# One output tile per attention step: spreading filler matmuls anew in a fused attention and FFN kernel on one Trainium2 core

## The chip, the core and the metric

The kernel runs on one core of one Trainium2 chip. The core has five engines that work beside each other and meet through semaphores: TensorE (PE in the profile; PEld is its loading of weights), VectorE (DVE), ScalarE (ACT), GpSimd (POOL) and SyncE (SP), which here only issues DMAs. Matrix products go to PSUM banks, all other tiles lie in SBUF, and inputs, outputs and some intermediates in HBM. The metric is the device time of one execution in microseconds, the median over runs.

## The reference

```python
def _A_ref(x, wqkv, wo):            # H = 32 heads of Dh = 16, S = 2048, D = 512
    q, k, v = (x @ wqkv) split in heads
    p = softmax(q k^T * Dh**-0.5)
    return (p v, heads joined) @ wo

def _B_ref(x, w_gate, w_up, w_down):   # F = 1792
    return (silu(x @ w_gate) * (x @ w_up)) @ w_down

xn = _layernorm(x)
s = _A_ref(xn, A_wqkv, A_wo)
g = silu(_B_ref(xn, B_w_gate, B_w_up, B_w_down))
return x + s * g
```

All data are fp32. Where TensorE multiplies, the kernel splits most operands in a high and a low part and sums three products (high by high, high by low, low by high).

## The kernel before

**Stages.** A prologue (to about 162 us of the span) normalises x, projects queries, keys and values, and writes them to HBM. Then comes the attention, 256 steps, in which everything else is hidden: the FFN and the output projection. A short tail ends it.

**The attention.** A unit `u` is four heads (`g` = u // 4) by one block of 512 queries (`b` = u % 4): 32 units of 8 steps each. The number of a step is `now = u * 8 + kp`, 0 to 255. A step handles 256 keys. On PE it issues, in program order (L801 to L823):

1. for `i = 0`: two score products `j = 0, 1` (L810, two matmuls each, into `score[0]` and `score[1]`), each followed by an exponential on ACT (L812). A score tile can be written again only when its exponential has read it;
2. `catch_up()`: what the last filler tile left to do (`after`), and then the value products of the *previous* step (`values(prev)`, L367, 16 records);
3. for `i = 1`: two more score products and exponentials;
4. `share()`: filler matmuls for this step;
5. if the previous step ended a unit, `finish` of that unit on DVE: transpose, reciprocal, product (L374 to L381), for odd `g` one more transpose (L388) and, for the last `g` and b > 0, a split into two parts (`split_o`, L261 and L262).

Step 0 has no value products, since nothing precedes it.

**The filler.** `queue` holds generators whose every `next` issues a *pair*: two matmuls of 64 rows into the banks `bankx` and `banky` (`both`, L174). Per FFN block there are 14 gate/up tiles of 24 pairs, in two groups (8 and 6), and after each group four down tiles of 24 or 18 pairs. Then come four tiles of 9 pairs for output block 3 (without its last part), and twelve output tiles of 12 pairs for blocks 0 to 2, here called O0 to O11. When a tile's last pair is issued, its readers follow in program order: a tanh on ACT (L203) and products on DVE (L204, L205) for a gate/up tile, adds on DVE (L222 to L227) for a down tile, and for an output tile the bank reads L340 and L341 on DVE, two products on POOL (L317, L318) and a store. The next tile writes the same two banks, so it waits until DVE has read them.

**The plan.** `plan()` writes the list `shares`: how many pairs each step issues. `tile_of(n, parts)` gives a tile of n pairs to that many steps in equal parts. `FIRST` pairs of the first step go between the scores of `i = 0` and `i = 1` (L816). A gate/up tile has 3 steps of 8. A down tile of 24 pairs has 3 steps of 8, or 2 of 12: `HALVED` counts sixteenths, so 9 of the 16 such tiles have two steps. `OUT_PARTS` gives the output tiles O0 to O10 one step of 12 or two of 6; O11 follows after the last step. All 256 steps have an entry. The first entries belong to tile 1, since tile 0 runs in the prologue.

**Work bound to a step's number.** `finish(29)` comes in step 240 and `finish(30)` in step 248. `load_gate` (L348), in step 248, loads four gate tiles and four tiles of x; `gate_rest` (L355 to L358), in step 251 and behind `share()`, runs eight operations on DVE with them. `out_steps` (L293) loads the parts of blocks 0 to 2 for the output tiles and splits them on DVE, two per step, when the queue has come so far; `load_gates` in it loads gates and x (L286, L287). `store_gate` and `next_out` (L176, L245) run in `catch_up` of the step after a down tile of the last group: a tanh on ACT (L178), a product on DVE (L179), the split of a part of `wo` (L241, L242) and of a part of block 3 (L261, L262), which the four tiles of 9 pairs read.

Of the kernel before, what the change touches and what calls it, by code (L numbers as in the profile page):

```python
# [25 lines left out]
NB = 4  # L26
TB = S // NB
NT = TB // P
DT = D // P
# [9 lines left out]
RING = NB + 1  # L39
DC = D // HALF  # L40
LIMIT = 160.0
FIRST = 5
HALVED = 9
OUT_PARTS = (2, 2, 1, 1, 1, 1, 1, 2, 1, 2, 2)
EPS = 1e-5
QSLOT = (0, 1, 0)
KSLOT = (0, 0, 1)
# [3 lines left out]
def tile_block(ctx: ExitStack, tc: tile.TileContext, x, wqkv, wo, w_gate, w_up, w_down, out):  # L51
# [51 lines left out]
    def load_k(g, c, i=None):  # L103
        load_rows(kst[(g * NB + c) % RING if i is None else i],
                  k_d[:, g * 64:(g + 1) * 64, c * TB:(c + 1) * TB], KSLOT)

    def load_q(u, i=None):
        g, b = divmod(u, NB)
        load_rows(qst[u % 2 if i is None else i], q_d[:, g * 64:(g + 1) * 64, b * TB:(b + 1) * TB], QSLOT)

    def load_shift(u):
        for h in range(2):
            sp.dma_start(qst[u % 2][h * HALF:h * HALF + 2].bitcast(F32),
                         sh_d.rearrange("(s u) (j h t) -> u h s j t", s=2, j=2, h=2)[u, h])

    def load_v(g, c):
        sp.dma_start(vst[(g * NB + c) % RING], v_d[g][:, c * CT:(c + 1) * CT])
# [38 lines left out]
    def catch_up():  # L156
        while after:
            after.pop(0)()
# [134 lines left out]
    def out_steps():  # L293
        for _ in range(min(2, len(splits))):
            b, c = splits.pop(0)
            split_o(lhs[b, c], parts_o[b, c])
            ready[b] += 1
        for b in range(NB - 1):
            if b not in stage and len(queue) <= (NB, NB, 2)[b]:
                for c in range(DT - 1):  # L300
                    load_out(b, c)
                stage[b] = now
            if b in stage and not b and (b, 1) not in stage and now > (u0 + b) * steps:
                load_out(b, DT - 1)
                stage[b, 1] = now
            if b in stage and (b, 2) not in stage and now > stage[b]:
                splits.extend((b, c) for c in range(DT - 1))
                stage[b, 2] = now
            if (b, 1) in stage and (b, 5) not in stage and now > stage[b, 1]:
                splits.insert(0, (b, DT - 1))  # L310
                stage[b, 5] = now
            if len(queue) <= NB - 1 - b and (b, 4) not in stage:
                load_gates(b)
                stage[b, 4] = now
# [33 lines left out]
    def load_gate():  # L348
        last.extend(on[:3] + [one.tile([P, D], F32, tag="wdr", name="last")])
        for t in range(NT):  # L350
            r = rows[(NB - 1) * NT + t]
            sp.dma_start(gate[t], g_d[r])
            sp.dma_start(last[t], x[r])

    def gate_rest():  # L355
        for t in range(NT):
            dve.scalar_tensor_tensor(facc[:, t], facc[:, t], 0.5, gate[t], op0=ALU.mult, op1=ALU.mult)
            dve.tensor_add(facc[:, t], facc[:, t], last[t])  # L358


    def values(item):
        u, kp, probs = item
        v, a = vst[(u // NB * NB + kp * 2 // CT) % RING], acc[u % 2]
        for i in range(2):
            kt = 2 * kp + i
            for h in range(4):
                mm(a[h * 32:h * 32 + DH + 1], v[:, kt % CT, h * (DH + 1):(h + 1) * (DH + 1)],  # L367
                   probs[2 * i + h // 2][:, h % 2], start=kt == 0, stop=kt == KT - 1, skip_group_check=True)
# [14 lines left out]
    def finish(u):  # L383
        g, b = divmod(u, NB)
        normalise(u, 0, TB)
        if g % 2:
            o2 = late.tile([P, TB], F32, tag="o2", name="o2")
            dve.transpose(o2, on[b])  # L388
            if g < NG - 1 or not b:
                (pool if g < NG - 1 else sp).dma_start(o_d[g // 2, b], o2)  # L390
            else:
                whole = (wd, hh)[b - 1].rearrange("p f j t -> p (f j) t")
                lhs[b, DT - 1] = whole[:, 2 * (DT - 1)], whole[:, 2 * DT - 1]
                split_o(lhs[b, DT - 1], o2)
                ready[b] += 1
# [14 lines left out]
    now = -1  # L410

    def fill(n):
        nonlocal given
        while n > 0 and not blocked():
            next(queue[0][1])
            queue[0][2] -= 1
            if not queue[0][2]:
                queue.pop(0)
            n -= 1
            given += 1  # L420
# [3 lines left out]
    shares = []  # L424

    def plan():
        def tile_of(n, parts):
            shares.extend([n // parts] * parts)

        halved = 0  # L430
        for i in range(2 * NB):
            nf = GROUPS[i % 2].stop - GROUPS[i % 2].start
            for _ in range(nf - (i == 0)):
                tile_of(3 * DC, 3)
            for t in range(NT):
                if nf == FG:
                    halved += HALVED
                    tile_of(3 * nf, 3 - halved // (NB * NT))
                    halved %= NB * NT
                else:  # L440
                    tile_of(3 * nf, 2)
        for _ in range(NT):
            tile_of(3 * (DT - 1), 1)
        for parts in OUT_PARTS:
            tile_of(3 * DT, parts)
        shares[0] -= FIRST

    def blocked():
        return not queue or queue[0][0] is not None and ready[queue[0][0]] < DT

    def share():
        if not blocked() and shares:
            fill(shares.pop(0))
# [337 lines left out]
    now = 0  # L791
    split_hidden()
    plan()
    prev = None

    exps = []
    settled = mybir.DependencyInfo(mybir.DependencyClass.Sync, mybir.DependencyReason.DATA)
    for u in range(units):
        g, b = divmod(u, NB)
        q = qst[u % 2]  # L800
        for kp in range(steps):  # L801
            now = u * steps + kp
            probs = []
            for i in range(2):
                kt = 2 * kp + i
                k, kc = kst[(g * NB + kt // CT) % RING], kt % CT
                for j in range(2):
                    for h in range(2):
                        r = slice(h * HALF, h * HALF + NROW)
                        mm(score[j][:, h], k[r, j, kc * P:(kc + 1) * P], q[r, j], start=True, stop=True)  # L810
                    pr = ppool.tile([P, 2, TB], F32, tag="pr", name="pr")
                    exps.append(act(pr, score[j], AF.Exp, scale=0.25))  # L812
                    if i == 0 and j == 1 and now:
                        tc.add_manual_dep(exps[-1].ins, exps[-3].ins.name, settled, reason="order of the slots' writes")
                    probs.append(pr)
                if now == i == 0:  # L816
                    fill(FIRST)
                if i == 0:
                    catch_up()
                if i == 0 and prev:  # L820
                    values(prev)
            old, prev = prev, (u, kp, probs)
            share()  # L823
            if old and old[1] == steps - 1:
                finish(old[0])
            if kp == 0:
                if u + 1 < units:
                    load_q(u + 1)
                    load_shift(u + 1)
            if g + 1 < NG and (b == 0 and kp == 0 or b == NB - 1 and kp in (2, 4, 6)):  # L830
                load_k(g + 1, kp // 2)
                load_v(g + 1, kp // 2)
            out_steps()
            if now == (units - 1) * steps:
                load_gate()
            if now == (units - 1) * steps + 3:
                gate_rest()
# [66 lines left out]
```

## Time and profile before

| | |
|---|---|
| three runs | 1448.03, 1449.05, 1448.93 us; median 1448.93 |
| profiled execution | 1448.02 us, span in the trace 1446.2 us |
| granted TensorE clock | 0.998 of full speed |
| exponentials (L812), mean of one | 1023 ns, 1024 of them |
| value products (L367), records | 4096 |
| filler matmuls of the gate/up tiles, mean of one | 392 ns |

In the views of the profile a line begins with the start in us from the span's start and the duration in us, then the engine, the line of the program (L810), the operation, and the tiles as out<-in. In brackets stands how long the engine was idle before it and what ended the idle time. The chain of waits is followed back from the last instruction; a row of it is a stretch in which that instruction set the pace. "PE bankx L174 x2" would be two filler matmuls. An engine with a q behind its name (SPq) is its instruction queue.

### The profile page before, as it was taken

The numbers are of one execution on the slowest core, as the hardware profiler recorded it, in microseconds if no ns is written. First come the engines' busy times: TensorE is split into PE (matmuls) and PEld (weight loads), VectorE is DVE, ScalarE is ACT, GpSimd is POOL, SyncE is SP. The second block draws the span as 40 slices with busy tenths as digits, with TensorE's granted clock in tenths as the row PEclk, the third lists the DMA queues.
The fourth block names the chain that finished last, engine by engine and source line by source line (L and its number), as shares of the span: only waits on it lengthen the run. The fifth ranks groups of instructions, "written<-read, shape, count | busy, mean of one in ns | idle before, by whom it ended". The sixth has DMA issues, their size and how long they took to land.

```text
span 1446.2 us, 26820 instructions
## 1 busy us (share of the span) xinstructions
PE 1430.6 (99%) x11237; PEld 804.3 (56%) x11237; DVE 538.9 (37%) x905; ACT 1110.2 (77%) x1235; POOL 88.7 (6%) x103
## 2 busy tenths in 40 slices
PE   8999999999999999999999999999999999999997
PEld 7777655555555555555555555555555555555554
DVE  6543344223423433134323431333253412434445
ACT  5733588778888888788888877888888877887774
POOL 3200200000000000000000000000000000000153
PEclk9999999999999999999999999999999999999999
DMA  6778652032264330242624311245424212315262
GB/s 209 265 243 243 162 118 62 23 80 69 71 150 118 96 78 20 49 107 71 143 67 127 80 42 34 78 107 112 116 67 125 56 25 47 83 36 173 76 202 78
DMA packets 127093, 148.64 MB, mean 103 GB/s; under 512 B 12540, under 2 KB 79100, under 8 KB 126196
## 3 DMA queue, kind: packets, MB, share of 16 engines
q1 hardware_dynamic: 121764, 126.19, 33.8%
q0 software_dynamic: 4912, 20.12, 3.8%
q8 instruction: 91, 1.49, 0.4%
q10 hardware_dynamic: 288, 0.52, 0.1%
q14 instruction: 38, 0.31, 0.1%
HBM read 106.94 MB, written 39.85 MB: 101 GB/s over the span
## 4 chain that ended last, share of the span: by engine, by line
PE 96%; ACT 2%; DVE 1%; issue 0%; DMA 0%; DVEq 0%; ACTq 0%
PE acc L367 32%; PE bankx L174 30%; PE score L810 20%; PE ps L578 6%; PE banky L174 4%; PE ps L580 3%; ACT pr L812 2%; PE acc L555 0%; PE bankx L330 0%; DMA facc<-in_A_x_dram 0%; DVE y L861 0%; DVE xn L550 0%; ACT xt L558 0%; DVE y L864 0%; PE bankx L585 0%
## 5 line engine op out<-in xcount | busy, mean ns | idle before, releaser
L812 ACT ACTIVATE pr<-score 128x1024 f32<-128x1024 f32 x1024 | 992.3, 1023 | 233.6 <-PE score L810 232.9
L367 PE MATMUL acc<-pr,vst 128*17 128x512 f32 x4096 | 489.2, 595 | 0.0
L810 PE MATMUL score<-qst,kst 50*128 50x512 f32 x2048 | 355.1, 422 | 3.4 <-ACT pr L812 2.4
L810 PEld LDWEIGHTS score<-qst,kst 50*128 50x128 f32 x2048 | 177.5, 185 | 268.4 <-ACT pr L812 230.6
L174 PE MATMUL bankx<-fx,guh 64*128 64x512 f32 x896 | 288.6, 392 | 0.0
L174 PE MATMUL banky<-fx,guh 64*128 64x512 f32 x896 | 288.6, 392 | 0.0
L367 PEld LDWEIGHTS acc<-pr,vst 128*17 128x17 f32 x4096 | 94.0, 97 | 235.7 <-issue 234.8
L204 DVE SCALAR_TENSOR_TENSOR ga<-th,bankx 128x512 f32<-128x512 f32 x56 | 38.5, 687 | 460.2 <-ACT th L203 460.2
L174 PEld LDWEIGHTS bankx<-fx,guh 64*128 64x128 f32 x896 | 165.9, 185 | 33.5 <-issue 0.3
L174 PE MATMUL banky<-fx,gul 64*128 64x512 f32 x448 | 175.4, 392 | 0.0
L174 PE MATMUL bankx<-fx,gul 64*128 64x512 f32 x448 | 175.4, 392 | 0.0
L174 PEld LDWEIGHTS banky<-fx,guh 64*128 64x128 f32 x896 | 166.0, 185 | 3.5
L174 PE MATMUL bankx<-wd,hh 64*128 64x512 f32 x672 | 165.5, 389 | 0.0
L174 PE MATMUL banky<-wd,hh 64*128 64x512 f32 x672 | 165.4, 389 | 0.0
L174 PEld LDWEIGHTS bankx<-wd,hh 64*128 64x128 f32 x672 | 124.1, 185 | 25.0
L174 PEld LDWEIGHTS banky<-wd,hh 64*128 64x128 f32 x672 | 124.2, 185 | 2.1
L174 PEld LDWEIGHTS bankx<-fx,gul 64*128 64x128 f32 x448 | 82.9, 185 | 17.7
L174 PEld LDWEIGHTS banky<-fx,gul 64*128 64x128 f32 x448 | 82.9, 185 | 1.7
L578 PE MATMUL ps<-xt,wh 128*128 128x512 f32 x256 | 80.7, 396 | 0.0
L135 DVE TENSOR_TENSOR gul<-gur,guh 128x1024 fp32r<-128x1024 f32 x56 | 68.6, 1225 | 2.4 <-DVE guh L134 0.5
L222 DVE COPY facc<-bankx 128x512 f32<-128x512 f32 x16 | 11.1, 691 | 153.1 <-PE banky L174 130.0
L390 POOL DMA_DIRECT2D o_d<-o x12 | 7.5, 622 | 824.7 <-DVE o L388 632.2
(147 smaller groups left out, 1065.0 us busy)
## 6 DMA issues: line engine op xcount, KB each, us to landing
gur<-in_B_w_gate_dram SPq DMA_DIRECT2D x56, 256.0 KB
gur<-in_B_w_up_dram SPq DMA_DIRECT2D x56, 256.0 KB
wdr<-in_B_w_down_dram SPq DMA_DIRECT2D x56, 256.0 KB
kst<-k_d SPq DMA_DIRECT2D x192, 64.0 KB
qst<-q_d SPq DMA_DIRECT2D x192, 64.0 KB
fx<-xt_d SPq DMA_DIRECT2D x24, 512.0 KB
q_d<-parts SPq DMA_DIRECT2D x16, 512.0 KB
k_d<-parts SPq DMA_DIRECT2D x16, 512.0 KB
```

The lines of the kernel that those rows point to most:

```text
L135: dve.tensor_sub(lo, raw, hi.bitcast(F32))
L174: mm(bank, lhs[h], rhs[h], start=start, stop=stop)
L204: dve.scalar_tensor_tensor(ga, th, 1.0, bankx, op0=ALU.add, op1=ALU.mult)
L222: dve.tensor_copy(facc[:, t], bankx)
L367: mm(a[h * 32:h * 32 + DH + 1], v[:, kt % CT, h * (DH + 1):(h + 1) * (DH + 1)], probs[2 * i + h // 2][:, h % 2], start=kt == 0, stop=kt == ...
L390: (pool if g < NG - 1 else sp).dma_start(o_d[g // 2, b], o2)
L578: mm(ps, w, a[:, c], start=n == 0, stop=n == 3 * DT - 1)
L580: mm(ps, a[:, c, tokens], w, start=n == 0, stop=n == 3 * DT - 1)
L810: mm(score[j][:, h], k[r, j, kc * P:(kc + 1) * P], q[r, j], start=True, stop=True)
L812: exps.append(act(pr, score[j], AF.Exp, scale=0.25))
```

## The change

Four places change, all in what is issued when; no instruction is added or removed.

```diff
-FIRST = 5
-HALVED = 9
-OUT_PARTS = (2, 2, 1, 1, 1, 1, 1, 2, 1, 2, 2)
+FIRST = (5, 2, 2)
+HALVED = 3
...
-            for _ in range(nf - (i == 0)):
-                tile_of(3 * DC, 3)
+            for f in range(nf - (i == 0)):
+                tile_of(3 * DC, 3 if i or f else 2)
...
-        for parts in OUT_PARTS:
-            tile_of(3 * DT, parts)
-        shares[0] -= FIRST
+        for _ in range(NB * NT - NT - 1):
+            tile_of(3 * DT, 1)
+        shares[0] -= sum(FIRST[:2])
+        shares[1] -= FIRST[2]
...
-                if now == i == 0:
-                    fill(FIRST)
+                    if now == i == 0 and j:
+                        fill(FIRST[0])
+                    elif (now, i, j) in ((0, 1, 0), (1, 0, 0)):
+                        fill(FIRST[1 + now])
```

The pairs per step, as the two plans give them (the entries of step 0 and 1 include those placed between scores):

| | before | after |
|---|---|---|
| tile 1 | steps 0 to 2: 8, 8, 8 | steps 0 and 1: 12, 12 |
| down tiles of 24 pairs in two steps | 9 of 16 | 3 of 16 |
| the last FFN tile ends in | step 235 | step 240 |
| block 3, four tiles of 9 | steps 236 to 239 | steps 241 to 244 |
| O0, O1 | 240, 241 and 242, 243 (6 each) | 245, 246 |
| O2 to O6 | 244 to 248 | 247 to 251 |
| O7 | 249, 250 (6 each) | 252 |
| O8 | 251 | 253 |
| O9, O10 | 252, 253 and 254, 255 (6 each) | 254, 255 |

In the opening, step 0 issues two scores, 5 pairs, a score, 2 pairs, a score, 5 pairs; step 1 a score, 2 pairs, a score, the value products of step 0, two scores, 10 pairs. Before, these were two scores, 5 pairs, two scores, 3 pairs; and two scores, the value products, two scores, 8 pairs.

Since the list of the steps' own work stays where it is, the filler tiles move past it: `finish(29)` now stands behind the last pair of the last FFN tile in DVE's program, and `gate_rest` behind O6 and one split, ahead of O7. In SP's program the load of the queries of unit 31 moves ahead of the loads for blocks 0 and 1, and the loads of the x rows for block 1 come to stand just before those of `load_gate`.

## The prediction

> **What bounds the kernel now.** I read the page first: busy times, then the chain that ended last.
>
> ```profile
> span 1446.2 us, 26820 instructions
> ...
> PE 1430.6 (99%) x11237; PEld 804.3 (56%) x11237; DVE 538.9 (37%) x905; ACT 1110.2 (77%) x1235; POOL 88.7 (6%) x103
> ...
> PE 96%; ACT 2%; DVE 1%; issue 0%; DMA 0%; DVEq 0%; ACTq 0%
> ```
>
> PE is the bound and the change removes none of its matmuls, so only stretches where PE waits can be won or lost. The chain in order of time, over the last hundred microseconds, shows what a step costs (a stretch that starts with "acc L367" is the value product of one step; from one to the next is one step).
>
> ```profile
> 1351.65 1.95 ACT pr L812 x2
> ...
> 1356.45 1.95 ACT pr L812 x2
> ...
> 1358.45 0.50 PE score L810 x2
> 1358.95 1.84 PE acc L367 x16
> 1360.79 0.45 PE score L810 x2
> ...
> 1361.26 1.95 ACT pr L812 x2
> ...
> 1374.31 1.84 PE acc L367 x16
> 1376.15 0.66 PE score L810 x4
> ...
> 1380.07 1.84 PE acc L367 x16
> ...
> 1412.30 0.46 PE score L810 x4
> ...
> 1424.69 1.95 ACT pr L812 x2
> ```
>
> A step with 12 pairs (1374.31 to 1380.07) takes 5.76 us and consists of PE alone: 1.84 for the values, 0.66 and 0.46 for the two groups of scores, 2.80 for the pairs. A step with 6 pairs (1356.45 to 1361.26) takes 4.81, and there the chain passes through two exponentials: the second score tile is not free until they end, and six pairs don't fill that time.
>
> The same view at the opening:
>
> ```profile
> 163.30 3.78 ACT pr L812 x4
> ...
> 167.63 1.84 PE acc L367 x16
> ...
> 172.47 1.84 PE acc L367 x16
> ...
> 177.31 1.84 PE acc L367 x16
> ```
>
> A step with 8 pairs takes 177.31 - 172.47 = 4.84. So a pair costs (5.76 - 4.84) / 4 = 0.23, a step without pairs 4.84 - 8 x 0.23 = 3.00, and six pairs would take 4.38 if PE set the pace. Since the steps (256) and the pairs stay the same in number, everything linear cancels: what counts is where a step is longer than 3.00 + 0.23 n.
>
> **1. The halved output tiles: a gain.** Nine steps of 6 pairs end in such a wait (first 1351.65, last 1424.69; the tenth, step 255, has no scores behind it). Each loses 4.81 - 4.38 = 0.43, together 3.9 us. Afterwards every step has at least 8 pairs. Those put into FFN down tiles make steps of 8, which run at PE's pace already. Bounds: 0 if another wait takes the same place, 3.9 if none does. I take 3.9, since the 12-pair and 8-pair rows show no exponential in the chain.
>
> **2. The pairs between scores at the opening: a gain.** No value product exists in step 0, and PE waits for exponentials:
>
> ```profile
> 165.29 0.18 PEld L810 LDWEIGHTS score<-qst,kst 50*128 50x128 f32 x2 [0.73 <-ACT pr L812]
> ...
> 167.12 0.19 PEld L810 LDWEIGHTS score<-qst,kst 50*128 50x128 f32 x2 [0.73 <-ACT pr L812]
> ...
> 173.05 1.23 DVE L135 TENSOR_TENSOR gul<-gur,guh 128x1024 fp32r<-128x1024 f32 x1
> 177.51 0.69 DVE L204 SCALAR_TENSOR_TENSOR ga<-th,bankx 128x512 f32<-128x512 f32 x1 [3.23 <-ACT th L203]
> 178.30 0.69 DVE L205 SCALAR_TENSOR_TENSOR ga<-ga,banky 128x512 f32<-128x512 f32 x1
> ```
>
> Ahead of the first value product stand 8 pairs now and 5 + 2 + 5 + 2 = 14 afterwards; six pairs are 1.39 us of work put into idle time. Going through the new order with these rows: the second score of step 0 still starts at 165.29 and streams for half of 0.46, five pairs run to about 166.8, a score and two pairs to 167.5, and the last score (free since the four exponentials ended at 167.08) to 167.7. The value product thus starts some 0.1 us later than 167.63: a gain of 1.3. Bounds: 0 if the delayed score holds the exponentials up by as much as is won, 1.39 at best.
>
> A cost comes with it. The first tile's 24 pairs now end in step 1 (10 pairs), and the next tile starts one step earlier: its first pair is due at 167.73 + 3.00 + 2.31 (next values, 173.04) + 1.84 + 0.66 = 175.54. The banks must have been read by L204 and L205 by then, and VectorE has L135 until 174.28; L204 and L205 after it take 178.99 - 177.51 = 1.48, so to about 175.7. With the restart I put 0.3 (0 if VectorE's order gives way, 0.8 if the weight load of the new tile is late too).
>
> **3. The end of the FFN meets the end of a unit: a loss.** Steps 240, 248 and 251 do fixed work by their number: `finish(29)`, `finish(30)`, `gate_rest`. The tiles move past them. The last down tile ended in step 235 and now ends in step 240, where `finish(29)` follows on VectorE, ahead of the next step's `store_gate` and `next_out`. Where VectorE stands, and PE's wait for it in the first output step of block 3:
>
> ```profile
> 1328.36 0.69 DVE L227 TENSOR_TENSOR y<-banky,y 128x512 f32<-128x512 f32 x1
> 1330.30 0.69 DVE L179 SCALAR_TENSOR_TENSOR y<-th,y 128x512 f32<-128x512 f32 x1 [1.25 <-ACT th L178]
> ...
> 1332.43 0.69 DVE L262 TENSOR_TENSOR part<-pair,part 128x512 fp32r<-128x512 f32 x1
> 1333.71 0.69 DVE L344 COPY facc<-bankx 128x512 f32<-128x512 f32 x1 [0.59 <-PE banky L174]
> ...
> 1340.18 0.42 DVE L261 CAST hh<-hh 128x512 fp32r<-128x512 f32 x1
> ...
> 1341.25 0.42 DVE L261 CAST hh<-hh 128x512 fp32r<-128x512 f32 x1
> ...
> 1352.44 0.71 DVE L374 STREAM_TRANSPOSE o<-acc 128x512 f32<-128x512 f32 x1
> ...
> 1355.75 0.42 DVE L261 CAST wd<-wd 128x512 fp32r<-128x512 f32 x1
> ...
> 1413.81 0.68 DVE L357 SCALAR_TENSOR_TENSOR facc<-facc,hh 128x512 f32<-128x512 f32 x1
> 1414.52 1.65 DVE L358 TENSOR_TENSOR facc<-facc,on 128x512 f32<-128x512 f32 x1
> 1416.10 1.76 DVE L357 SCALAR_TENSOR_TENSOR facc<-facc,hh 128x512 f32<-128x512 f32 x1
> ...
> 1421.58 0.69 DVE L340 TENSOR_SCALAR y<-bankx 128x512 f32<-128x512 f32 x1 [0.33 <-PE banky L174]
> 1422.38 0.69 DVE L341 SCALAR_TENSOR_TENSOR y<-banky,y 128x512 f32<-128x512 f32 x1
> ```
>
> ```profile
> PEld bankx L174 <- DVE part L261: 1.0, 1, 1.0
> ```
>
> PE waited 1.0 us there already, for the split of L261/L262 whose end (1333.12) releases the last pair. `finish` with its split takes 1355.75 - 1352.44 = 3.31. VectorE was free at about 1328.97 (0.61 after L227's start, as its operations follow each other) and idle until the tanh came; with `finish` in that place L179 starts at 1332.28 instead of 1330.30. All behind it, and PE's wait, move by 1.98: a loss of 2.0. Bounds: 1.3 (part of it beside PE's own work) to 3.3 (all of `finish`).
>
> **4. `gate_rest` stands before a bank release that has no second step left: a loss.** In step 251 it runs behind tile O8 and takes 1421.58 - 0.33 - 1413.81 = 7.44 until VectorE asks for O9, which takes two steps: nobody waited. Afterwards it runs behind O6, with one more split (1341.25 - 1340.18 = 1.07) ahead of it, and O7 ends one step of 5.76 later. With step 251's pairs ending at 1412.30: O7 ends at 1418.06, its release L340 could start at 1418.17, but VectorE comes to it at 1413.81 + 1.07 + 7.44 = 1422.3 and has read the second bank 0.80 + 0.69 later, at 1423.8. PE wants the banks for O8 at 1418.06 + 0.46 + 1.84 + 0.66 = 1421.0. From the end of such a split to the end of the pair behind it row 1333.71 shows about 0.48, so O8's first pair ends near 1424.3 instead of 1421.25: a loss of 2.9 (with the unrounded rows). What is late next is only O8's own release, with a full step for 1.5 us of work.
>
> Lower bound 0.9: two of the eight operations took 1.65 and 1.76 instead of 0.69, beside these on POOL.
>
> ```profile
> 1413.98 1.65 POOL L317 TENSOR_TENSOR y<-y,gates 128x512 f32<-128x512 f32 x1 [2.69 <-DVE y L341]
> 1415.71 1.61 POOL L318 TENSOR_TENSOR pair<-y,pair 128x512 f32<-128x512 f32 x1
> ```
>
> Without those 2.0 us the loss is 0.9. The upper bound, 4, has the loads of rival B a microsecond late. I take 2.9, as POOL does the same two products for O6 at the same place. [...]
>
> POOL's own work, 1.65 + 1.61 at most for a tile, fits a 5.76 step, so one tile a step doesn't make POOL the bound.
>
> **Sum.** -3.9 - 1.3 + 0.3 + 2.0 + 2.9 = 0.0. The profiled execution took 1448.02 (span 1446.2 and 1.8 around it), the median of the runs is 0.9 above it: I predict 1448.9. Each wait removed comes back as a wait on VectorE.
>
> **The rivals.**
>
> A, the VectorE waits don't appear: only 1 and 2 count, 1448.9 - 5.2 = 1443.7. For it: VectorE is busy only 37%. Against it: the order of its instructions puts `finish(29)` and `gate_rest` ahead of the operations PE waits for, and in the rows above its operations follow their program order. Chance 0.15.
>
> B, slower: `gate_rest` waits for its loads. The gate and x rows are queued on SP behind the load of x for the next block, which waits for an output store:
>
> ```profile
> 1386.62 0.33 SPq L287 DMA_DIRECT2D pair<-in_A_x_dram  x1
> ```
>
> That came 7.0 after O3 ended (0.46 before 1380.07). O3 now ends in step 248, where `load_gate` is issued, so the eight loads leave behind it; `gate_rest` starts 3 x 5.76 + 2.6 = 19.9 after O3. This leaves 12.9 us for eleven loads. From the point where they need more, every microsecond is one of PE: 4 us late gives 1452.9. Chance 0.12.
>
> C, the opening gives nothing because the exponentials of step 1 are pushed back by what PE wins: 1448.9 + 1.3 = 1450.2, still no change. Chance 0.10.
>
> [...] Chance 0.08.
>
> **How the numbers follow.** The forecast keeps 0.55, with a range of its own of 1447 to 1450.5 from the bounds of 2, 3 and 4. I give 1445.0 to 1451.5, which takes in C and D and leaves out A and B but for their mild ends. What this measurement can tell from no change is about 0.2%, 2.9 us: below 1446.0 is faster, A and a tail of the forecast, 0.17; above 1451.8 is slower, B, 0.12; no change is 0.71.
>
> **What would show it.** Right: no step with an exponential in the chain among the output steps; the first value product near 167.7 with 14 pairs ahead; PE waiting about 3 us for L262's counterpart in step 241, and about 3 us for VectorE's bank reads in step 253, behind a run of eight `gate_rest` operations. Wrong: step 241 or 253 at its plain length (A), `gate_rest` waiting on a DMA (B), the first value product after 168.5 (C), or output steps above 5.8 us throughout, which would mean that POOL or the loads can't follow one tile a step.

## The result and the profile after

| | before | after |
|---|---|---|
| median, 16 runs each | 1448.2 us (1447.68 to 1449.05) | 1451.95 us (1447.5 to 1453.15) |
| span of the profiled execution | 1446.2 us | 1450.8 us |
| granted TensorE clock in it | 0.998 | 0.995 |

The ratio after to before is 1.002, with a 95% interval of 1.0014 to 1.0027: slower by 3.75 us, 0.26%, and 0.45 us above the stated range. The 16 runs after fall into three groups: two took 1447.5 and 1447.65 us, with a granted clock of 0.999, two about 1449.4 with 0.998, and twelve 1450.9 to 1453.15 with 0.995 or 0.996.

The page of the changed kernel, the same rows as before:

```profile
span 1450.8 us, 26829 instructions
...
PE 1434.1 (99%) x11237; PEld 807.6 (56%) x11237; DVE 540.2 (37%) x905; ACT 1111.1 (77%) x1235; POOL 88.0 (6%) x103
...
PE 97%; DVE 2%; ACT 0%; issue 0%; DMA 0%; DVEq 0%
```

The exponentials (ACT, 2% before) are gone from the chain and VectorE (DVE) went from 1% to 2%. PE is busy 3.5 us longer with the same 11237 instructions, so some of them ran slower.

The chain of waits in order of time, through steps 241 and 242:

```profile
1343.18 0.63 DVE o L373
...
1345.79 0.69 DVE wd L261
1346.48 0.60 DVE y L178
1347.09 0.35 DVE fx L240
1347.43 0.02 issue
1347.46 0.69 DVE fx L241
1348.15 0.35 DVE part L260
1348.50 0.04 issue
1348.54 0.79 PE bankx L173
1349.33 0.42 PE bankx L173
1349.76 0.42 PE bankx L173
1350.19 0.85 PE score L810 x4
1351.04 3.54 PE acc L366 x16
1354.58 0.82 PE score L810 x3
1355.40 0.23 PE banky L173
...
1357.97 1.84 PE acc L366 x16
```

The first half is the wait that part 3 of the prediction describes: `finish(29)` (L373 to L261), then L178, the split of `wo`, and the split that PE needs (L260). The second half was not described: behind it a pair takes 0.42 instead of 0.23, the values 3.54 instead of 1.84, and from 1355.40 on a pair again 0.23.

The busy time by stretches shows why (columns: stretch, its length, busy us and instructions of PE, PEld, DVE, ACT and POOL, the granted clock of PE, the share of the DMA engines, GB/s):

```profile
1341.00:1348.00 7.00, 5.03 (x42) 2.36 (x38) 6.00 (x11) 4.72 (x6) 0.54 (x1) 1.00 0.80 265
1348.00:1355.00 7.00, 6.46 (x28) 2.41 (x30) 2.56 (x5) 1.94 (x2) 0.00 (x0) 0.51 0.49 188
1355.00:1362.00 7.00, 7.00 (x62) 4.34 (x60) 3.44 (x6) 5.60 (x6) 0.00 (x0) 1.00 0.00 0
1410.00:1416.50 6.50, 6.50 (x56) 3.60 (x52) 6.39 (x7) 4.14 (x5) 3.32 (x3) 1.00 0.66 214
1416.50:1419.50 3.00, 0.77 (x5) 0.18 (x1) 2.84 (x5) 1.94 (x2) 0.00 (x0) 1.00 0.06 22
1419.50:1423.00 3.50, 3.47 (x18) 2.71 (x20) 0.00 (x0) 0.00 (x0) 3.06 (x3) 0.53 0.43 150
1423.00:1430.00 7.00, 7.00 (x61) 4.30 (x57) 1.40 (x3) 3.88 (x4) 3.22 (x4) 0.99 0.25 93
```

The granted clock is half from 1348.06 to 1354.89, and again from 1419.74 to 1423.15. Ahead of each such stretch PE waited: 5.03 of the 7 us before 1348 are busy, and only 0.77 of the 3 us before 1419.5. The same view of the kernel before has the clock at 1.00 throughout this part:

```profile
1325.00:1440.00 115.00, 111.84 (x878) 58.75 (x876) 57.71 (x91) 80.63 (x86) 38.42 (x35) 1.00 0.39 128
```

The page's row of 40 slices hides this, because a slice is 36 us long and shows "9" for anything from 0.9 up.

The second place in the order of VectorE's operations, step 251:

```profile
1409.55 0.42 DVE L260 CAST hh<-hh 128x512 fp32r<-128x512 f32 x1
1410.01 1.65 DVE L261 TENSOR_TENSOR hh<-hh 128x512 fp32r<-128x512 f32 x1
1411.58 1.78 DVE L356 SCALAR_TENSOR_TENSOR facc<-facc,hh 128x512 f32<-128x512 f32 x1
...
1417.39 0.69 DVE L357 TENSOR_TENSOR facc<-facc,last 128x512 f32<-128x512 f32 x1
1418.00 0.68 DVE L339 TENSOR_SCALAR y<-bankx 128x512 f32<-128x512 f32 x1
1418.78 0.69 DVE L340 SCALAR_TENSOR_TENSOR y<-banky,y 128x512 f32<-128x512 f32 x1
```

From the split to the release of O7's first bank it is 1418.00 - 1409.55 = 8.45 us; forecast were 1.07 + 7.44 = 8.51. None of these operations waits for a load.

The opening, in the chain: 

```profile
168.09 1.84 PE acc L366 x16
...
173.38 1.84 PE acc L366 x16
...
178.29 1.82 PE acc L366 x13
```

The second value product comes 173.38 - 172.47 = 0.91 us later than before, with 24 instead of 16 pairs done (1.85 us of pairs). From it to the third, step 2 takes 4.91, 0.07 over its plain length.

### The profile page after: what moved, and what is told of

Read it like the earlier page. It is cut to its first block, busy times and chain, and to the rows that moved or that the text cites. A ratio compares the mean times of both kernels' runs of the same rounds, so it can differ in the third digit from the quotient of the medians.

```text
span 1450.8 us, 26829 instructions
## 1 busy us (share of the span) xinstructions
PE 1434.1 (99%) x11237; PEld 807.6 (56%) x11237; DVE 540.2 (37%) x905; ACT 1111.1 (77%) x1235; POOL 88.0 (6%) x103
## 4 chain that ended last, share of the span: by engine, by line
PE 97%; DVE 2%; ACT 0%; issue 0%; DMA 0%; DVEq 0%
PE acc L366 32%; PE bankx L173 30%; PE score L810 20%; PE ps L578 6%; PE banky L173 5%; PE ps L580 3%; PE acc L555 0%; DVE facc L356 0%; PE bankx L329 0%; DMA facc<-in_A_x_dram 0%; DVE y L863 0%; DVE xn L550 0%; ACT xt L558 0%; DVE y L866 0%; DVE y L339 0%
```

## The experiments

**The question.** Theory: a PE wait of about 3 us is followed by a stretch at half clock, and that is what the forecast lacks. Rival: the clock falls late in the kernel for another reason, for instance the denser 12-pair steps, and the waits cost only their length. The times of the kernel before, run beside these experiments, have medians of 1447.9 to 1448.0.

**gate_spread: no wait in step 253.**

```diff
-    def gate_rest():
-        for t in range(NT):
+    def gate_rest(t):
...
-            if now == (units - 1) * steps + 3:
-                gate_rest()
+            if 0 <= now - (units - 1) * steps - 3 < NT:
+                gate_rest(now - (units - 1) * steps - 3)
```

> The changed kernel with gate_rest taken apart: two of its eight operations in each of the steps 251 to 254 instead of all in step 251. Theory (a PE wait of about 3 us makes the granted clock fall to half for one or two stretches of 3.4 us, and that is the part of the loss that was not forecast): step 253 takes its plain 5.76 us instead of 10.32, the half clock after 1419 is gone while the one after 1348 stays; 1451.95 - 4.6 = about 1447.4 us, granted clock 0.997 to 0.998. Rival (the clock falls late in the kernel for another reason, for instance the denser 12-pair steps, whatever PE waits for): only the wait itself of 2.9 us goes, about 1449.1 us, and the clock still falls near 1420.

Measured: 1446.73 us (1444.87 to 1447.9), ratio to the kernel before 0.999 (0.9981 to 0.9999). That is 5.2 us less than the changed kernel. In the attention its trace has one stretch at half clock left, from 1351.19 to 1354.61, behind the wait of step 241 (another stands in the prologue, see the last section). The rival's 2.9 us is too little.

**finish_later: a shorter wait in step 241.**

```diff
-            if old and old[1] == steps - 1:
+            if now == (units - 2) * steps + 1:
+                finish(units - 3)
+            elif old and old[1] == steps - 1 and now != (units - 2) * steps:
                 finish(old[0])
```

> The changed kernel with finish(29) issued in step 241 behind the filler pairs instead of in step 240, so that it no longer stands ahead of the split that PE waits for. Theory: step 241 goes from 8.91 back to about 6.1 us and step 242 from 6.93 to 5.06, the half clock after 1348 is gone, the one in step 253 stays: 1451.95 - 4.6 = about 1447.3 us. Rival: only the longer wait of 2.0 us goes, about 1450.0 us, with the clock at half at the same place as before.

Measured: 1447.22 us (1446.01 to 1448.55), 4.7 us less, ratio 0.9994 (0.9985 to 1.0003). As with gate_spread, the loss that goes is larger than the wait. Its trace has no half clock behind step 241 and, as expected, one stretch in step 253, from 1413.54 to 1420.37.

**both_moved.** Both edits.

> Both edits at once. Theory: no stretch at half clock is left before the tail, every step but 241 (about 6.1) at its plain length: 1451.95 - 9.2 = about 1442.8 us, granted clock 0.998 or more, and the runs no longer spread over 5 us. Rival: 1451.95 - 2.0 - 2.9 = about 1447.1 us with a granted clock of 0.995 to 0.996.

Measured: 1443.18 us (1443.04 to 1444.24), 8.8 us less than the changed kernel and 4.8 less than the one before: ratio 0.9969 (0.9957 to 0.9981). The runs lie within 1.2 us, and the clock over the span:

```profile
core 0: 1441.3 us, clock 0.999
```

The 12-pair steps are all still there and its trace has no half clock ahead of the tail, so they don't lower the clock.

**kept_busy: the waits stay, PE works in them.** This tells the wait from what follows it.

```diff
+            for _ in range({241: 11, 253: 12}.get(now, 0)):
+                mm(acc[(u + 1) % 2], fx[:, 0, 0, :P], fx[:, 0, 0], start=True, stop=True, skip_group_check=True)
             share()
```

> The changed kernel with matmuls added whose results nobody reads (128x512 into the idle acc bank): 11 ahead of the pairs of step 241 and 12 ahead of those of step 253, about as long as PE waits there. VectorE's order, and so the moment at which PE may go on, stays as it is. Theory: the same 3 us are lost in each of the two steps, but PE is busy in them, so the clock does not fall: step 242 at 5.06 and step 253 at about 8.7; 1451.95 - 4.3 = about 1447.6 us, granted clock 0.998. Rival: the clock falls all the same, 1452 us or more.

Measured: 1448.03 us (1447.6 to 1449.24), ratio 1.0001 (0.9992 to 1.001). Its chain at step 241 has the added matmuls (L826) where the wait was, and behind them, from the second pair on, nearly all pairs and the values at their usual length:

```profile
1341.95 1.84 PE acc L366 x16
1343.80 0.67 PE score L810 x4
1344.46 2.70 PE acc L826 x11
1347.16 0.42 PE bankx L173
...
1350.07 1.84 PE acc L366 x16
```

```profile
1348.00:1355.00 7.00, 7.00 (x60) 3.88 (x56) 2.68 (x5) 3.93 (x5) 0.00 (x0) 1.00 0.44 167
1414.00:1420.00 6.00, 6.00 (x40) 4.62 (x40) 2.53 (x5) 1.65 (x2) 2.94 (x3) 1.00 0.36 114
```

Step 241 still lasts 1350.07 - 1341.95 = 8.12 us, 3.06 over its plain 5.06, but the clock stays at 1.00. There is more work on PE and 1451.95 - 1448.03 = 3.9 us less time: about this much was the clock.

**before_wait1h, before_wait2, before_wait3: the wait by itself, in the kernel before.** VectorE gets 0.61, 1.07 or 2.14 us of repeated work in step 236, ahead of the split that PE waits for: `n` below is 1 in before_wait2 and 2 in before_wait3, and before_wait1h repeats only the subtraction of the split.

```diff
     def next_out(t):
+        for _ in range(n if t == DT - 1 else 0):
+            split_wo(t)
         split_wo(t)
```

> The kernel before with one more VectorE subtraction (0.61 us) ahead of the split that PE waits for in step 236: a wait of about 1.7 us. If the clock falls only behind waits of 2 us and more: 1448.0 + 0.6 = about 1448.6 us and the granted clock as before. If a wait of 1.7 us is enough in some runs: these runs at 0.997 and over 1450 us.

> The kernel before with the split of wo in step 236 done twice, so that VectorE is 1.07 us later and PE waits about 2.1 us there instead of 1.0. If a wait of 2 us leaves the clock alone: 1448.0 + 1.1 = about 1449.1 us. If it halves it, 1450.5 us or more, with a granted clock of 0.996 to 0.997.

> The same with the split done three times: PE waits about 3.2 us in step 236, as long as in step 241 of the changed kernel. Theory: the clock falls to half behind it in most runs and the loss is 2.1 for the wait and 1.7 to 2.7 for the clock, 1451.8 to 1452.8 us; the runs spread over several us. Rival: 2.1 alone, about 1450.1 us.

The wait of the weight load in the three traces, in this order:

```profile
PEld bankx L174 <- DVE part L263: 1.7, 1, 1.7
```

```profile
PEld bankx L174 <- DVE part L263: 2.2, 1, 2.2
```

```profile
PEld bankx L174 <- DVE part L263: 3.4, 1, 3.4
```

Measured: 1448.99 us (1448.35 to 1450.0) with a ratio of 1.0007 (0.9998 to 1.0016); 1450.12 (1448.96 to 1451.17) with 1.0015 (1.0005 to 1.0024); and 1452.37 (1451.62 to 1453.18) with 1.003 (1.0019 to 1.004). The first loses about what it waits, 0.95 us for a wait 0.7 us longer; the only half clock in its trace ahead of the tail is in the prologue. The third loses 4.5 us for 2.1 us of added work; its trace has 3.4 us at half clock behind the wait:

```profile
1337.00:1340.40 3.40, 3.40 (x20) 0.49 (x16) 1.36 (x2) 1.94 (x2) 0.00 (x0) 0.50 0.40 154
```

The second is undecided as a whole: four of its eleven runs took 1448.96 to 1449.34, the wait alone, and five 1450.5 or more; the other two, at 1449.9 and 1450.12, can't be told. Its profiled execution (span 1447.6) is one of the former, without half clock behind the wait.

**opening_alone, outputs_moved: the two gains by themselves.** The first has the change's `FIRST` and tile 1 in two steps, `HALVED = 8`, and the old `OUT_PARTS`. The second is the kernel before with these lines and the edits of both_moved:

```diff
-HALVED = 9
-OUT_PARTS = (2, 2, 1, 1, 1, 1, 1, 2, 1, 2, 2)
+HALVED = 4
+OUT_PARTS = (1,) * 11
```

> The kernel before with only the opening of the change: 14 instead of 8 pairs ahead of the first value product, tile 1 in two steps; one down tile of the second half of an early block goes from two steps to three, so that the later steps stand where they stood. Forecast of part 2: -1.3 + 0.3, so about 1447.0 us, the first value product later by 0.1 and the second by 0.7, with 8 pairs more done. Rival C: no difference, 1448.0 us.

> The kernel before with the output tiles in one step each and 4 instead of 9 sixteenths of the down tiles in two steps, its opening unchanged, and with the edits of both_moved so that no wait on VectorE is added: part 1 of the prediction alone. Forecast: -3.9, about 1444.0 us, with no step longer than its plain length but 241 (about 6.1). Rival (a second wait takes the place of the exponentials'): 1446 us or more.

Measured: 1446.95 us (1446.62 to 1447.78) beside 1447.87, so -0.9, ratio 0.9993 (0.9984 to 1.0002, which does not exclude no change); and 1444.2 us (1443.7 to 1444.96) beside 1448.04, so -3.8, ratio 0.9974 (0.9964 to 0.9985).

**no_waits: the best version.** both_moved, and in step 241 the split comes first:

```diff
-                                after.append(partial(next_out, t))
+                                after.insert(0 if t == NT - 1 else 1, partial(next_out, t))
...
     def next_out(t):
+        if t == DT - 1:
+            split_o(lhs[NB - 1, t - 1], plain[t - 1])
         split_wo(t)
...
-        else:
+        elif t < DT - 1:
             split_o(lhs[NB - 1, t - 1], plain[t - 1])
```

> The kernel of both_moved, and in step 241 the split that PE waits for is issued ahead of the product of store_gate and of the split of wo. Theory: the 1.1 us that step 241 still lost goes too, and every step from 2 on runs at PE's pace: 1443.2 - 1.1 = about 1442.1 us. Rival (PE then waits for something else in that step, the tanh that now comes later or the queue of loads): 1443 us or more.

Measured: 1442.7 us (1441.93 to 1442.87), ratio 0.9961 (0.9946 to 0.9975): 5.2 us faster than the kernel before and 9.2 faster than the changed one. Step 241 in its chain, from one value product to the next:

```profile
1342.75 1.84 PE acc L367 x16
...
1347.82 1.84 PE acc L367 x16
```

5.07 us, its plain length. The median is only 0.5 below both_moved, not 1.1; its profiled execution, at 1442.85, had a stretch at half clock in the prologue (last section), and two of the five runs took 1441.93 and 1441.96.

## Why the prediction was wrong

| term | forecast | measured | by |
|---|---|---|---|
| 1, halved output tiles | -3.9 | -3.8 | outputs_moved |
| 2, opening, with its stall | -1.3 + 0.3 | -0.9 | opening_alone |
| 3 and 4, length of the two waits | +2.0 + 2.9 | +4.8 | kept_busy (+0.04 in all), less the two rows above |
| half clock behind the waits | none | +3.9 | after less kept_busy |
| sum | 0.0 | +3.75 to +4.0 | |

The third row of the table is what kept_busy leaves over, so that the sum closes by construction; the lengths have their own readings. In the trace of gate_spread the half clock starts only at the end of step 241, which lasts 1351.06 - 1342.97 = 8.09 us (starts of its value products in the timeline). In the kernel before, the step with this wait, 236, lasts 6.14: 1.95 more, where 1.98 was forecast. For step 253 the 8.45 us above stand against 8.51.

**Right:** parts 1, 3 and 4 as mechanisms and as lengths (the rows of part 4 give 1424.3 - 1421.25, about 3.0 and not 2.9, which changes nothing). Part 2 is right in its total only: the first value product came 168.09 - 167.63 = 0.46 us later in these traces instead of 0.1, and the stall in step 2 was 0.07 instead of 0.3. That these two errors cancel is luck. Rivals A and B did not occur. Against C stands the trace: the third value product comes 0.98 us later with 8 more pairs (1.85 us) done; the time of opening_alone by itself doesn't exclude C. D, a loss of 0.9 instead of 2.9 in part 4 (chance 0.08), did not occur either: L261 and L356 beside POOL took 1.65 and 1.78 us, as taken there. The trace after doesn't show these two at 0.69, nor does the trace before (1.65 and 1.76). By their times and clocks (0.999), the changed kernel does come out at no change where no stretch at half clock falls: two of its runs, at 1447.5 and 1447.65, and kept_busy at 1448.03. The forecast's base of 1448.9 was also 0.7 above the median of the 16 runs before.

**The step that failed** is in the sum: "Each wait removed comes back as a wait on VectorE." The forecast priced a wait of PE at its length and put at nothing what the wait does to the work behind it. Behind the two waits that work ran at half clock, by their granted clock of 0.995 or 0.996 in twelve of the 16 runs, and this cost 3.9 us in the median. Step 242 is no part of any term, and yet it took 1357.97 - 1351.04 = 6.93 us instead of 5.06. The rows quoted for step 236, where PE waits 1.0 us without any such effect, gave no sign of it, while the two waits that the change makes are longer (the weight loads' waits in the trace after: who waited for whom, us in total, times, the longest):

```profile
PEld bankx L173 <- DVE part L260: 2.9, 1, 2.9
...
PEld bankx L173 <- DVE y L339: 2.4, 1, 2.4
```

The second bank of step 253 is read another 0.8 us later. The nine waits that went, of 0.43 us each, had stood in a kernel whose clock showed no half stretch between them (1.00 from 1325 to 1440 us), so they gave back only their length.

What the traces show of it: the clock is at 0.50, for 3.41 us (after, from 1419.74 on) or twice that (after, 6.83 us from 1348.06 on), and it didn't fall at the same moment of the wait in two traces. The wait in step 241, 2.9 us in the trace after, brought half clock there from 1348.06 on, before it had ended, and in gate_spread only from 1351.19 on, behind it. By their times and clocks, twelve runs of the changed kernel seem to have the loss twice, two once and two not at all. The prediction could have had it as a rival: in the tail of the trace before the clock is at 0.50 from 1441.62 us on, behind 3.41 us with PE busy for 1.20. As PE has no work behind that, the trace doesn't show what it costs.

**How idle PE was ahead of it.** The kept traces show it roughly. Each stretch at half clock behind a wait is one or two times 3.41 us long, and the 64.85 us between the two of the changed kernel are 19 times 3.413. In the rows with half clock the stretch is the 3.41 us just ahead of it. In the two others it is an estimate: the 3.41 us that hold most of the wait, counted on in such steps from another change of the clock in the same trace.

| trace, step | stretch | PE busy in it | clock in the next |
|---|---|---|---|
| after, 253 | 1416.33 to 1419.74 | 1.15 | half |
| before_wait3, 236 | 1333.61 to 1337.02 | 1.31 | half |
| after, 241 | 1344.65 to 1348.06 | 1.38 | half |
| finish_later, 253 | 1410.13 to 1413.54 | 1.55 | half |
| before_wait2, 236 | 1330.90 to 1334.31 | 1.68 | full |
| gate_spread, 241 | 1347.78 to 1351.19 | 1.74 | half |
| before_wait1h, 236 | 1330.29 to 1333.70 | 2.44 | full |

So PE was idle for 1.67 to 2.26 of the 3.41 us ahead of each of the five falls. The half clock lasted twice as long where the wait reached into its first 3.41 us, with PE busy for 2.93 of them (after, step 241) and for 3.31 (finish_later), but not where PE was busy in all of them (3.41 in after, step 253). A stretch of 3.41 us cost 1.66 us (step 242 of gate_spread, 6.72 instead of 5.06), one of twice that 2.7 (in the trace after step 241 lasts 1350.97 - 1342.06 = 8.91, 0.82 more than the 8.09 of the wait alone, and step 242 1.87 more than plain).

**Left open:** the exact share. Waits of 1.0 and 1.7 us showed no loss beyond their length, 2.2 us gave mixed runs, 3.4 us a loss in every run. 1.68 and 1.74 us in the table stand in the wrong order, so if the estimated stretch is right, PE's busy time alone doesn't decide. In the prologue of the trace before, 3.41 us with PE busy for 1.90 (4.61 to 8.02) were followed by full clock. Why runs of one kernel differ is not shown: that the clock falls at another moment of the wait in each is the author's estimate, from the 1348.06 and 1351.19 above.

## What to carry to other kernels

In these kernels TensorE is the bound, and its waits of 2.4 to 3.4 us cost more than their length, because the clock halved behind them in most runs. That added 1.7 us for 3.41 us at half clock and 2.7 for twice that (3.9 in the median for the two waits of the changed kernel), and matmuls without a use in place of the wait avoided it (kept_busy, clock 1.00). Look at the granted clock in stretches of a few microseconds, as the slices of 36 us didn't show it here. Before filler work is moved past operations that are bound to a step's number, write down the order of the releasing engine at the new meeting points; here moving two groups of VectorE operations by one to three steps turned a loss of 3.75 us into a gain of 4.8.

## What was not expected of the hardware

The same happens in the prologue, in five of the twelve profiled executions. The kernels before_wait2 and before_wait3 are alike up to step 236; the first has its clock at 1.00 throughout the prologue, the second at half for 3.4 us near the start, with PE busy 1.65 us of the 3.2 us ahead of it:

```profile
6.00:9.20 3.20, 1.65 (x10) 0.92 (x9) 2.56 (x5) 2.05 (x4) 2.26 (x3) 1.00 1.04 349
9.20:12.60 3.40, 3.40 (x8) 2.68 (x9) 2.90 (x8) 0.29 (x2) 2.26 (x2) 0.51 1.08 294
```

Their first value products start at 167.76 and 168.49 us. The other traces agree: with the old opening the first value product starts at 167.39 to 167.76 in three traces without such a stretch and at 168.44 and 168.49 in two with it; with the new opening at 167.76 to 168.16 in four without and at 168.63 to 169.25 in three with it. These 0.7 us are most of the 1 us by which runs of kernels without long waits differ; no experiment took the stretch away, so the cause is read from traces and not tried.
